# Nine-token rows for keys and values, per-head v transfers and a new order of the first chunk in a polysketch attention kernel

## The chip, the cores and the metric

The kernel runs on one core of a Trainium2 chip. The metric is device time in microseconds, from the start to the end of one execution; three runs of the kernel before gave 110.10, 110.65 and 111.04, a median of 110.65. A core has TensorE (PE in the profile, its weight loads apart as PEld), VectorE (DVE), ScalarE (ACT), GpSimd (POOL) and SyncE (SP), which here only issues transfers. Each engine works through its own instructions in the order of the program, and waits for the others through semaphores.

## What is computed

Two blocks follow each other. The first is attention with polynomial sketches, for 4 batches of 4 heads, 1088 tokens and 32 channels, with sketches of r = 8 rows:

```python
def phi(x):
    a = np.einsum('rd,bhsd->bhsr', S1, x)
    b = np.einsum('rd,bhsd->bhsr', S2, x)
    return np.einsum('bhsi,bhsj->bhsij', a, b).reshape(*x.shape[:-1], r * r)
q_p, k_p = phi(q), phi(k)
kv = np.einsum('bhsf,bhsd->bhfd', k_p, v)
z = np.sum(k_p, axis=2)
num = np.einsum('bhsf,bhfd->bhsd', q_p, kv)
den = np.einsum('bhsf,bhf->bhs', q_p, z)[..., None] + 1e-06
```

Its quotient num / den, with the heads side by side, is x, of 4 x 1088 x 128. The second block is x + relu(norm(x) @ w_ch1) @ w_ch2, where norm takes the mean and the deviation over 128 channels and scales by g_ln, and the hidden width is 512. All arrays are 32-bit floats on the chip, apart from S1, S2, w_ch1 and w_ch2, which arrive as 64-bit floats and are put together from their two 32-bit words by shifts, masks and float operations.

## The kernel before

**Layout.** A batch of q, k or v is seen as 128 rows of 34 tokens (4 heads x 32 rows, 34 = 1088 / 32), row by row on the partitions. q and k are loaded so (`load_rows`, L97), 544 KB a batch, the first batch of k in two pieces of 18 and 16 tokens. The 34 tokens of a row are cut into 9, 9, 8 and 8 (`ST`, `SN`), so that a batch's tokens, for one head, fill 9 tiles of 128, the last of them half empty. `turn_k` (L265) turns k by 32 x 32 blocks on VectorE into `kT`, channels on partitions; it works on two of the four cuts at a time. For batch 0 the four cuts lie on every fourth column (`step=4`), for later batches in blocks of 32. `load_v` (L104) brings v in the same order of tokens onto the partitions, by four transfers a batch, one a cut, each onto 32 partitions for all heads; a head has 10 tokens' room in a partition, and the ninth is zeroed first (L116).

**Sketches.** S1 and S2 are loaded sixteen times over, onto all 128 partitions (L79), one by ACT's queue and one by SP's. VectorE makes floats of them (`s_f`, L188 to L202); `sketches` (L279) makes `sk` for the keys and, by GpSimd, `sq` for the queries; `sketches2` (L293) makes `s2b`.

**Attention of a batch.** `key_features` (L308): matmuls of kT with sk, copied to `fs` by ACT. `key_products` (L327): the outer product of the two sketches, on GpSimd and for a third of batch 0 on VectorE. `key_sums` and `key_scale` (L337, L349) put the sum z into the query's sketch. `key_values` (L355): 36 matmuls of v with the products, nine tiles by four heads, head by head within a tile, so its first four need all heads of v. `key_rows` and `key_spread` (L365, L371) lay the result out as `kvr`. On the query's side: `turn_q`, `query_features`, `query_rows`, `quotients`, `query_products`, `query_turn`, then `numerators` (L454).

**Second block.** It goes by chunks of 512 tokens, two a batch, and a last one (8) of what is left over. `columns_of(c)` has x with channels on partitions; `send` stores it and `fetch` loads it back in rows for `stats` and the residual (chunk 0 is turned by TensorE instead, `turn_rows`). `hidden(c, j)` (L537), four a chunk, is a matmul with w1 and ACT's relu; `second(c, t)` (L548), four a chunk, has four matmuls with w2 each; `finish(c)` (L561) scales, adds x and stores.

**Weights.** The class `weight` (L210) makes floats of w1 and w2 in steps: `split` on VectorE (exponents and mantissa bits, `ex` and `bits`), `floats(0..3)` on ACT, `add` on GpSimd, `exps` on GpSimd (the exponents of W2), `signed` and `last` on VectorE. W1 is done in halves of 256, apart from its split and its step 3. `mean_free(a, bank)` (L580) is a matmul of `cg` and W1's half, which takes the mean out of w1; ACT copies the result to `w1`.

**Order.** Nothing is planned by a scheduler: the order is written out by hand, for chunk 0 from L583 on. `fill` (L162) is a matmul of ones that nobody reads, into the bank `XP` = `M[2]`, to keep TensorE going. The loads of batch 1 (L609 to L612) are released by a one-element copy into `kn[1]` on GpSimd (L608), which waits for `query_rows(0, 0, 4)`. In SP's queue the loads stand in the order S2, k (two), q, w1, v (four), w2, then k, q, v of batch 1 and k of batch 2, and from there on chunk by chunk between stores and fetches.

Of the kernel before, what the change touches and what calls it, by code (L numbers as in the profile page):

```python
# [25 lines left out]
def kernel(  # L26
# [29 lines left out]
    ST, SN = (0, 9, 18, 26), (9, 9, 8, 8)  # L56
# [13 lines left out]
    XP = M[2]  # L70
# [6 lines left out]
    s_raw = const([P, 2 * D], S1.dtype, "s_raw")  # L77
    for eng, src, a in ((act, S1, 0), (nc.sync, S2, D)):
        eng.dma_start(out=s_raw[:, a : a + D],  # L79
                      in_=bass.AP(src.tensor, src.offset, [[0, P // R], [D, R], [1, D]]))  # L80
# [7 lines left out]
    act.dma_start(out=g_row, in_=moe_g_ln.rearrange("(o p) -> o p", o=1))  # L88
# [3 lines left out]
    VH = 10 * D  # L92
# [4 lines left out]
    def load_rows(dst, src, b, t0=0, t1=G):  # L97
        nc.sync.dma_start(
            out=dst[b][:, D * t0 : D * t1],
            in_=bass.AP(src.tensor, src.offset + b * H * S * D + D * t0,  # L100
                        [[G * D, P], [1, D * (t1 - t0)]]),
        )

    def load_v(b):  # L104
        base = v.offset + b * H * S * D
        for r in range(4):
            n = SN[r] * D
            nc.sync.dma_start(
                out=_ap(vn[b], *((r, 32) if b == 0 else (32 * r, 32)), 0, [[VH, H], [1, n]],
                        step=4 if b == 0 else 1),  # L110
                in_=bass.AP(v.tensor, base + ST[r] * D, [[G * D, 32], [S * D, H], [1, n]]),
            )


    for t in vn:
        (dve if t is vn[0] else pool).memset(_ap(t, 0, P, 8 * D, [[VH, H], [1, D]]), 0.0)  # L116
    load_rows(kn, k, 0, 0, 18)
    load_rows(kn, k, 0, 18, G)
# [6 lines left out]
    )  # L125

# [19 lines left out]
    dve.tensor_tensor(out=m8, in0=bit, in1=head, op=ALU.is_equal)  # L146
    kT = [const([P, NT * P], F32, f"kT{i}") for i in range(2)]
    for t in kT:
        pool.memset(t[:, 8 * P :], 0.0)
# [38 lines left out]
    s_f = const([P, 2 * D], F32, "s_f")  # L188
    if s_raw.dtype == F32:
        dve.tensor_copy(out=s_f, in_=s_raw)  # L190
    else:
        t = exponent(s_raw, P, 2 * D, "s")
        split(t)
        act.activation(t["mant"], t["bits"], AF.Identity, bias=one, scale=2.0**-20)
        dve.tensor_scalar(out=t["exf"], in0=t["ex"], scalar1=-896.0, scalar2=0.0,
                          op0=ALU.add, op1=ALU.max)
        dve.tensor_scalar(out=t["e2"], in0=t["exf"], scalar1=255.0, scalar2=2.0**23,
                          op0=ALU.min, op1=ALU.mult)
        signed(t)
        dve.scalar_tensor_tensor(out=t["mant"], in0=t["lo"], scalar=2.0**-52, in1=t["mant"],  # L200
                                 op0=ALU.mult, op1=ALU.add)
        dve.tensor_tensor(out=s_f, in0=t["mant"], in1=t["e3"].bitcast(F32), op=ALU.mult)  # L202
# [7 lines left out]
    class weight:  # L210


        def __init__(self, dst, raw, tag):
            self.dst, self.raw, self.plain = dst, raw, raw.dtype == F32
            if not self.plain:
                self.t = exponent(raw, P, raw.shape[-1], tag)

        def cols(self, a, n):
            return {k: x[:, a : a + n] for k, x in self.t.items()}
# [17 lines left out]
        def exps(self, a=0, n=512):  # L237
            if not self.plain:
                t = self.cols(a, n)
                pool.tensor_scalar(out=t["exf"], in0=t["ex"], scalar1=-896.0, scalar2=0.0,  # L240
                                   op0=ALU.add, op1=ALU.max)
                pool.tensor_scalar(out=t["e2"], in0=t["exf"], scalar1=255.0, scalar2=2.0**23,
                                   op0=ALU.min, op1=ALU.mult)
# [18 lines left out]
    W1, W2 = weight(w1g, w1_raw, "w1"), weight(w2, w2_raw, "w2")  # L262


    def turn_k(b, r2):  # L265
        n = SN[r2]
        at, dims = (r2, [[1, 2], [P, n], [4, 32]]) if b == 0 else (
            32 * r2, [[32, 2], [P, n], [1, 32]])
        dve.transpose(  # L269
            _ap(kT[b % 2], 0, P, at, dims),  # L270
            _ap(kn[b], 0, P, D * ST[r2], [[D * n, 2], [D, n], [1, D]]),
        )
# [6 lines left out]
    def sketches():  # L279

        s_t = const([P, W], F32, "s_t")
        dve.transpose(s_t, s_f)
        dve.tensor_tensor(
            out=_ap(sk, 0, P, 0, [[HR, 2], [R, H], [1, R]]),
            in0=_ap(s_t, 0, P, 0, [[HR, 2], [R, H], [1, R]]),
            in1=_ap(m32, 0, P, 0, [[0, 2], [1, H], [0, R]]),
            op=ALU.mult,
        )
        for b in range(B):
            pool.tensor_copy(out=_ap(sq[b], 0, P, 0, [[R, 2], [1, R]]),  # L290
                             in_=_ap(s_t, 0, P, 0, [[HR, 2], [1, R]]))

    def sketches2():  # L293

        dve.tensor_tensor(
            out=_ap(s2b, 0, P, 0, [[D, H], [1, D]]),
            in0=_ap(s_f, 0, P, D, [[0, H], [1, D]]),
            in1=_ap(m8, 0, P, 0, [[1, H], [0, D]]),
            op=ALU.mult,
        )  # L300
# [279 lines left out]
    def mean_free(a, bank):  # L580
        pe.matmul(bank[:, 0:half], cg, w1g[:, a : a + half], start=True, stop=True)

    fill(2, XP, 512)  # L583
    turn_k(0, 0)
    sketches()
    turn_k(0, 2)
    fill(1, XP, 512)
    pe.matmul(FB[:, 64:65], g_row, one[0:1], start=True, stop=True)
    act.copy(g_col, FB[:, 64:65])
    pool.tensor_scalar(out=cg, in0=ident, scalar1=-1.0 / DM, scalar2=g_col,  # L590
                       op0=ALU.add, op1=ALU.mult)
    sketches2()
    key_features(0, 0, 4, M[0])
    key_features(0, 4, 9, M[1])
    key_products(pool, 0, 0, 4)
    turn_q(0, 0, 4)
    fill(1, XP, 256)
    key_sums(0, FB, 0)
    fill(1, XP)
# [3 lines left out]
    fill(1, XP)  # L603
    query_features(0, 0, 4)
    W1.split()
    query_rows(0, 0, 4)

    pool.tensor_copy(out=kn[1][:, 0:1], in_=fq[0][:, 0:1])  # L608
# [4 lines left out]
    W1.floats(3)  # L613
    W1.floats(2, 0, half)
    W1.add(0, half)
    W1.floats(0, 0, half)
    W1.floats(1, 0, half)
    W1.floats(0, half, half)
    quotients(0, 0, 4)
    fill(1, XP, 512)  # L620
    fill(1, XP, 256)
    key_values(0)
    key_rows()
    W1.floats(1, half, half)
    fill(1, XP, 256)
    key_spread(0, M[0], 0)
# [3 lines left out]
    query_turn(0, 2, 2)  # L630
    W1.signed(0, half)
    W1.last(dve, 0, half)
    W1.floats(2, half, half)
    W1.add(half, half)
    W2.floats(3)
    fill(1, XP, 512)
    numerators(0, 0, 4)
    columns_of(0)
    mean_free(0, M[0])
    act.copy(w1[:, 0:half], M[0][:, 0:half])  # L640
    W1.signed(half, half)
    W1.last(dve, half, half)
    W2.split()
    W2.exps()
    turn_q(0, 4, 4)
    W2.floats(2)
    fill(1, XP)


    pool.memset(kT[0][:, 8 * P + 64 :], 0.0)  # L650
    hidden(0, 0)
    W2.add()
    mean_free(half, FB)
    act.copy(w1[:, half:], FB[:, 0:half])
    query_features(0, 4, 4)
    hidden(0, 1)
    W2.signed()
    query_rows(0, 4, 4)
    turn_k(1, 0)
    W2.last(dve)  # L660
    turn_rows(0)
# [3 lines left out]
    turn_k(1, 2)  # L665
# [31 lines left out]
    turn_k(2, 0)  # L697
    turn_k(2, 2)
# [33 lines left out]
    for b in range(1, 4):  # L732
# [37 lines left out]
        if b < 2:  # L770
            turn_k(b + 2, 0)
            turn_k(b + 2, 2)
# [78 lines left out]
```

## Time and profile before

| what | value |
|---|---|
| median of three runs | 110.65 us (110.10 to 111.04) |
| profiled execution | 110.73 us, of which the span from first to last instruction is 108.9 us |
| instructions in it | 3605 |
| granted TensorE clock | 0.996 of full speed |
| bytes read and written in HBM | 9.77 MB, 4.19 MB |
| DMA issue to landing, median: q, k, v, w | 5.5, 6.3, 5.1 (v's larger pieces), 6.6 us |
| first chunk: `key_values(0)`, numerators, `hidden(0,0)`, `second(0,0)` start at | 13.12, 17.17, 19.31, 25.88 us |

All times of the profile are microseconds from the span's start. In a line of the profile stand the engine, the line of the kernel, the operation, the tile written and the tiles read, the shape, and how often; in brackets the idle time of the engine before it and what ended it. A row of digits cuts the span into 40 slices of 2.7 us, with the busy share of each in tenths. A matmul of 32-bit floats appears as two records. The engine lists count busy time only; transfers are listed by queue, with their packets.

### The profile page before, as it was taken

To read this page: it belongs to the slowest core of one execution; us is meant where nothing else is said; L and a number is where in the kernel's file an instruction comes from. 1 tells how busy PE (TensorE), PEld (TensorE's weight loads), DVE (VectorE), ACT (ScalarE), POOL (GpSimd) and SP (SyncE) were. 2 spreads that over 40 slices of the span, in tenths; PEclk is the share of its full clock that TensorE was granted. 3 is DMA by queue.
4 is the path that set the end of the run, shared out by engine and by line. 5 is a ranking of instruction groups with operands and counts; after the bars stand their busy time and mean duration, and the time that the engine had idled before them with its cause. 6 is when DMAs were issued, how large, how long until landed. Compare 5 with 4: busy or idle time off the path is not lost. (4 is left out here: it accounts for less than half of the span.)

```text
span 108.9 us, 3605 instructions
## 1 busy us (share of the span) xinstructions
PE 100.2 (92%) x1496; PEld 67.3 (62%) x1496; DVE 70.9 (65%) x204; ACT 39.2 (36%) x79; POOL 53.9 (49%) x67
## 2 busy tenths in 40 slices
PE   6949996994999999999999999999999999999890
PEld 3317545445973677836963786559449658849680
DVE  5496989349859958789879703896950493274411
ACT  4103693662222532434316511451282251071220
POOL 7036682992997397672960693059340034016000
PEclk9999999999999999999999999999999999999998
DMA  1999159910002595334495862520036450132031
GB/s 24 251 332 360 62 174 341 264 45 3 6 0 102 155 303 149 143 106 124 82 355 181 204 211 76 152 56 17 3 76 219 122 163 11 48 91 53 0 96 48
DMA packets 12162, 14.19 MB, mean 130 GB/s; under 512 B 2417, under 2 KB 8946, under 8 KB 12146
## 3 DMA queue, kind: packets, MB, share of 16 engines
q1 hardware_dynamic: 11856, 13.87, 42.8%
q8 instruction: 11, 0.18, 0.7%
q10 hardware_dynamic: 290, 0.10, 0.3%
q14 instruction: 5, 0.04, 0.1%
HBM read 9.77 MB, written 4.19 MB: 128 GB/s over the span
## 5 line engine op out<-in xcount | busy, mean ns | idle before, releaser
L552 PEld LDWEIGHTS M<-w,hT 128*128 128x128 f32 x256 | 31.0, 191 | 7.7 <-issue 3.8
L552 PE MATMUL M<-w,hT 128*128 128x128 f32 x256 | 34.3, 281 | 1.5 <-DVE w L260 1.4
L542 PE MATMUL M<-xT,w 128*128 128x512 f32 (+1 forms) x72 | 34.2, 588 | 0.7 <-DVE ob L564 0.5
L544 ACT ACTIVATE hT<-M 128x512 f32<-128x512 f32 (+1 forms) x36 | 20.6, 574 | 33.7 <-PE M L542 33.7
L432 POOL TENSOR_TENSOR qp<-a,fq 128x1024 f32<-128x1024 f32 (+1 forms) x9 | 16.2, 1816 | 20.0 <-DVE a L425 20.0
L564 DVE SCALAR_TENSOR_TENSOR ob<-M,rstd,x 128x128 f32<-128x128 f32 x32 | 9.0, 344 | 16.5 <-PE M L552 7.1
L542 PEld LDWEIGHTS M<-xT,w 128*128 128x128 f32 x72 | 11.9, 189 | 9.9 <-issue 6.6
L330 POOL TENSOR_TENSOR kp<-fs 128x1024 f32<-128x1024 f32 (+2 forms) x8 | 16.2, 2036 | 2.2 <-ACT fs L324 1.4
L443 DVE STREAM_TRANSPOSE qpT<-qp 128x1024 f32<-128x1024 f32 (+1 forms) x10 | 10.8, 1082 | 4.0 <-POOL qp L432 3.9
L164 PE MATMUL M<-ones 128*128 128x512 f32 (+2 forms) x22 | 10.5, 591 | 1.1 <-DVE ones L86 1.1
L524 POOL TENSOR_SCALAR va<-mv 128x4 f32<-128x4 f32 (+1 forms) x9 | 2.1, 229 | 15.8 <-DVE mv L517 15.6
L526 POOL TENSOR_TENSOR rstd<-va,mhalf 128x4 f32<-128x4 f32 (+1 forms) x9 | 9.0, 1000 | 0.7
L461 PE MATMUL X<-qpT,kvr 32*32 32x256 f32 (+2 forms) x384 | 7.5, 323 | 1.0 <-DVE qpT L443 1.0
L515 DVE BATCH_NORM_STATS2 st<-x 128x6 f32<-128x128 f32 x34 | 7.4, 279 | 0.3
L461 PEld LDWEIGHTS X<-qpT,kvr 32*32 32x32 f32 x384 | 4.5, 103 | 4.4 <-ACT loww L235 1.8
L269 DVE STREAM_TRANSPOSE kT<-kn 128x576 f32<-128x576 f32 (+1 forms) x8 | 6.4, 822 | 1.0 <-DMA kn<-in_k_dram 1.0
L476 ACT COPY xT<-X 128x512 f32<-128x512 f32 (+1 forms) x8 | 4.2, 561 | 7.7 <-PE X L461 7.7
L164 PEld LDWEIGHTS M<-ones 128*128 128x128 f32 x22 | 4.4, 226 | 4.1 <-issue 2.7
L409 DVE STREAM_TRANSPOSE fq<-X 128x512 f32<-128x512 f32 (+1 forms) x9 | 5.8, 669 | 1.0 <-PE X L399 1.0
L507 DVE STREAM_TRANSPOSE x<-xx 128x512 f32<-128x512 f32 (+1 forms) x8 | 5.4, 669 | 0.8 <-DMA xx<-xd 0.8
L358 PEld LDWEIGHTS FB<-kp,vn 128*32 128x32 f32 x288 | 4.2, 110 | 2.6 <-POOL kp L330 1.5
L387 DVE STREAM_TRANSPOSE qT<-qn 128x1024 f32<-128x1024 f32 (+1 forms) x5 | 5.1, 1015 | 0.6 <-DMA qn<-in_q_dram 0.6
(100 smaller groups left out, 85.5 us busy)
## 6 DMA issues: line engine op xcount, KB each, us to landing
qn<-in_q_dram SPq DMA_DIRECT2D x4, 544.0 KB, 5.5
out_dram<-ob SPq DMA_DIRECT2D x33, 64.0 KB, 1.8
xd<-xT SPq DMA_DIRECT2D x7, 256.0 KB, 2.6
xx<-xd SPq DMA_DIRECT2D x28, 64.0 KB, 2.0
kn<-in_k_dram SPq DMA_DIRECT2D x3, 544.0 KB, 6.3
vn<-in_v_dram SPq DMA_DIRECT2D x8, 144.0 KB, 5.1
w_raw<-in_moe_w_ch_dram SPq DMA_DIRECT2D x2, 512.0 KB, 6.6
vn<-in_v_dram SPq DMA_DIRECT2D x8, 128.0 KB, 5.8
```

Of the source, the lines that this page charges most:

```text
L164: pe.matmul(bank[:, 0:w], ones, _ap(ones, 0, P, 0, [[0, w // P], [1, P]]), start=True, stop=True)
L269: dve.transpose(_ap(kT[b % 2], 0, P, at, dims), _ap(kn[b], 0, P, D * ST[r2], [[D * n, 2], [D, n], [1, D]]),)
L330: eng.tensor_tensor(out=_ap(o, 0, P, H * F * t0, [[F, (t1 - t0) * H], [R, R], [1, R]]), in0=_ap(a, 0, P, at, [[R, (t1 - t0) * H], [1, R], ...
L432: eng.tensor_tensor(out=_ap(qp[p, t0 // 4], 0, P, H * F * (t0 % 4), [[F, m], [R, R], [1, R]]), in0=_ap(a2s[p], 0, P, HR * t0, [[R, m], [1, ...
L443: dve.transpose(_ap(qpT[p], 0, P, 32 * t0, [[32, n], [width(p), 8], [1, 32]]), qp[p, t0 // 4][:, o : o + n * H * F],)
L461: pe.matmul(X[D * h : D * h + D, 512 * r + 32 * t0 : 512 * r + 32 * (t0 + n)], kvr[p if p < 4 else r][rows, DM * i + D * h : DM * i + D * ...
L515: dve.bn_stats(out=st[:, 6 * t : 6 * t + 6], in_=x[c][:, P * t : P * (t + 1)])
L526: pool.tensor_tensor(out=rs[:, 0:n], in0=va[:, 0:n], in1=mhalf[:, 0:n], op=ALU.pow)
L542: pe.matmul(hp[:, 0:n], w1[:, P * j : P * (j + 1)], xT[c][:, 0:n], start=True, stop=True)
L544: act.activation(_ap(hT[c], 0, P, 512 * j, dims), hp[:, 0:n], AF.Relu)
L552: pe.matmul(po[c][:, DM * t : DM * (t + 1)], hT[c][:, 512 * j + P * t : 512 * j + P * (t + 1)], w2[:, DM * j : DM * (j + 1)], start=(j == ...
L564: dve.scalar_tensor_tensor(out=ob[c][:, P * t : P * (t + 1)], in0=po[c][:, P * t : P * (t + 1)], scalar=rstd[c][:, t : t + 1], in1=x[c][:, ...
```

## The change

- **Rows of nine tokens.** All four cuts of a row are nine tokens: 0 to 8, 9 to 17, 18 to 26 and 27 to 35. The last has only seven of its own; for v the other two are read from what follows, and `kT` is zero there (its padding is now two tiles of 32 columns, zeroed once). Batch 0 has the same layout as the others, and k of batch 0 comes by one transfer. `turn_k` takes ranges of cuts and tokens.
- **v by heads.** `load_v` has one transfer a head, onto all 128 partitions; its source is 4 cuts x 32 rows x 288 numbers. For the last head of the last batch it is two transfers, and the piece that would be read past the end is zeroed instead. The other zeroing of v is gone.
- **Sketches.** S1 and S2 go onto every fourth partition (32 in all), both by SP's queue, after a memset of `s_raw` on GpSimd; the conversion is 32 wide instead of 64. `s2b` now needs S on each partition, which a matmul with a new 0/1 matrix `pick` (made by a GpSimd iota and one VectorE comparison) puts into `M[2]`. g's load moves behind ACT's table load, its matmul to just before.
- **W1 in halves.** `split` and step 3 of W1 are done by halves too; for the first half `ex` and `bits` lie in the PSUM bank `M[0]`. W2's `exps` go to VectorE, the copy of w1's first half too.
- **Order of chunk 0.** Fills go to X, and those between `query_features(0)` and `key_values(0)` are gone. `cg` is made later. The copy that releases batch 1's loads is on ACT, behind `key_spread(0)`, and waits for the quotients. `mean_free` of the second half and `turn_k(1)` stand later, W2's steps earlier.

```diff
-    VH = 10 * D
+    VH = NT * D
...
     def load_v(b):
-        base = v.offset + b * H * S * D
-        for r in range(4):
-            n = SN[r] * D
-            nc.sync.dma_start(
-                out=_ap(vn[b], *((r, 32) if b == 0 else (32 * r, 32)), 0, [[VH, H], [1, n]],
-                        step=4 if b == 0 else 1),
-                in_=bass.AP(v.tensor, base + ST[r] * D, [[G * D, 32], [S * D, H], [1, n]]),
-            )
+        for h in range(H):
+            at = v.offset + (b * H + h) * S * D
+            parts = [(0, 3, NT), (3, 4, 7)] if (b, h) == (B - 1, H - 1) else [(0, 4, NT)]
+            for r0, r1, n in parts:
+                nc.sync.dma_start(
+                    out=_ap(vn[b], 32 * r0, 32 * (r1 - r0), VH * h, [[1, D * n]]),
+                    in_=bass.AP(v.tensor, at + r0 * NT * D,
+                                [[NT * D, r1 - r0], [G * D, 32], [1, D * n]]),
+                )
...
-    for eng, src, a in ((act, S1, 0), (nc.sync, S2, D)):
-        eng.dma_start(out=s_raw[:, a : a + D],
-                      in_=bass.AP(src.tensor, src.offset, [[0, P // R], [D, R], [1, D]]))
+    pool.memset(s_raw.bitcast(U32), 0)
+    for src, a in ((S1, 0), (S2, 1)):
+        nc.sync.dma_start(out=_ap(s_raw, a, H * R, 0, [[1, D]], step=4),
+                          in_=bass.AP(src.tensor, src.offset, [[0, H], [D, R], [1, D]]))
...
-    load_rows(kn, k, 0, 0, 18)
-    load_rows(kn, k, 0, 18, G)
+    load_rows(kn, k, 0)
...
+            if self.bank is not None and a == 0:
+                y = self.bank.bitcast(U32)
+                t["ex"], t["bits"] = y[:, 0:n], y[:, n : 2 * n]
...
-                pool.tensor_scalar(out=t["exf"], in0=t["ex"], scalar1=-896.0, scalar2=0.0,
-                                   op0=ALU.add, op1=ALU.max)
+                dve.tensor_scalar(out=t["exf"], in0=t["ex"], scalar1=-896.0, scalar2=0.0,
+                                  op0=ALU.add, op1=ALU.max)
...
-    def turn_k(b, r2):
+    def turn_k(b, r0, r1, t0, t1):
+        n = t1 - t0
         dve.transpose(
-            _ap(kT[b % 2], 0, P, at, dims),
-            _ap(kn[b], 0, P, D * ST[r2], [[D * n, 2], [D, n], [1, D]]),
+            _ap(kT[b % 2], 0, P, 32 * r0 + P * t0, [[32, r1 - r0], [P, n], [1, 32]]),
+            _ap(kn[b], 0, P, D * (NT * r0 + t0), [[D * NT, r1 - r0], [D, n], [1, D]]),
         )
```

The order of chunk 0 after the change, from its first fill to `hidden(0, 0)`:

```python
    fill(2, X, 512)
    sketches()
    turn_k(0, 0, 4, 0, 4)
    dve.tensor_scalar(out=pick, in0=away, scalar1=0, scalar2=None, op0=ALU.is_equal)
    turn_k(0, 0, 3, 4, 9)
    turn_k(0, 3, 4, 4, 7)
    fill(1, X, 256)
    key_features(0, 0, 4, M[0])
    key_products(pool, 0, 0, 4)
    turn_q(0, 0, 4)
    pe.matmul(M[2][:, 64:65], g_row, one[0:1], start=True, stop=True)
    sketches2(M[2])
    key_features(0, 4, 9, M[1])
    fill(1, X)
    key_sums(0, FB, 0)
    fill(1, X)
    key_scale(0, FB, 32)
    key_products(pool, 0, 4, 6)
    key_products(dve, 0, 6, 9, M[1], 4)
    W1.split(0, half)
    fill(1, X)
    query_features(0, 0, 4)
    W1.floats(3, 0, half)
    query_rows(0, 0, 4)
    for step in (2, 0, 1):
        W1.floats(step, 0, half)
...
    quotients(0, 0, 4)
    key_values(0)
    key_rows()
    W1.floats(3, half, half)
    fill(1, X, 256)
    key_spread(0, M[1], 0)
    act.copy(kn[1][:, 0:1], a2s[0][:, 0:1])
    load_rows(kn, k, 1)
    load_rows(qn, q, 1)
    load_v(1)
    load_rows(kn, k, 2)
    query_products(0, pool, 2, 2)
    query_products(0, dve, 0, 2)
    query_turn(0, 0, 2)
    query_turn(0, 2, 2)
    W1.add(0, half)
    W1.signed(0, half)
    W1.last(dve, 0, half)
    W1.split(half, half)
    W2.floats(3)
    fill(1, X, 512)
    fill(1, X, 256)
    numerators(0, 0, 4)
    columns_of(0)
    for step in (2, 0, 1):
        W1.floats(step, half, half)
    mean_free(0, M[0])
    dve.tensor_copy(out=w1[:, 0:half], in_=M[0][:, 0:half])
    turn_q(0, 4, 4)
    W1.add(half, half)
    W2.split()
    W1.signed(half, half)
    W1.last(dve, half, half)
    W2.exps()
    W2.signed()
    fill(1, M[2])
    hidden(0, 0)
```

## The prediction

> **What bounds the kernel now.** I read the busy times first, then the chain of waits, then the timeline from the start to 30 us, the windows of 1 us over the same stretch, and the DMA lists.
>
> ```profile
> PE 100.2 (92%) x1496; PEld 67.3 (62%) x1496; DVE 70.9 (65%) x204; ACT 39.2 (36%) x79; POOL 53.9 (49%) x67
> PE   6949996994999999999999999999999999999890
> ```
>
> TensorE is the bound. From 25.88 us on its timeline has hardly a hole, so whatever delays or advances the stretch before it moves the end by the same amount. The chain of waits starts only at 102.77 us and says nothing of the head; the head is where the change works. Its timeline:
>
> ```profile
> 13.12 1.21 PE L358 MATMUL FB<-kp,vn 128*32 128x64 f32 x72
> 16.31 0.71 DVE L443 STREAM_TRANSPOSE qpT<-qp 128x512 f32<-128x512 f32 x1 [0.22 <-POOL qp L432]
> 17.17 1.06 PE L461 MATMUL X<-qpT,kvr 32*32 32x128 f32 x64 [1.04 <-DVE qpT L443]
> 19.31 1.13 PE L542 MATMUL M<-xT,w 128*128 128x512 f32 x2 [0.24 <-ACT w L640]
> 25.88 2.02 PE L552 MATMUL M<-w,hT 128*128 128x128 f32 x16 [1.36 <-DVE w L260]
> 27.83 1.27 PE L315 MATMUL X<-sk,kT 128*64 128x64 f32 x36
> ```
>
> `key_values(0)` runs at 13.12, behind fills and not behind v. The numerators wait for VectorE's second transpose (done 17.02), `hidden(0,0)` for the first half of w1 (19.31), `key_features(1)` starts at 27.83. I follow 19.31: from there to 27.83 are 8.5 us.
>
> **The start.** S1 moves from ACT's queue to SP's, behind a new GpSimd memset (0.72 us, about 0.2 us by the memset rows), and k becomes one transfer. By the 0.69 and 0.64 us of SP's issues k goes out at about 2.2 instead of 1.46, but q and w1 only 0.1 later. S lands at 4.0 instead of 3.1; the conversion (1.3 us) and `sk` are done by 5.8, before k (6.4), so k hides them; without that cover they would cost 0.9. The first turn writes whole blocks: 0.71 us as L269 in its later runs, against 1.20 here. First features at 7.2 instead of 8.00. The rest of kT (two turns, 0.9 us), `pick` (0.2 to 0.3), `turn_q` (q lands at 8.6 as now, 0.71) and `s2b` (0.27) bring VectorE to 9.6, where its key products stood at 9.77: the 0.8 is mostly lost again. The `pick` matmul and g's move onto M2 lie in TensorE's holes.
>
> **W1.** Its two splits took 0.78 and 1.30 us at 512 wide beside GpSimd's products; W2's, with less beside them, 0.42. For a half written to PSUM I bound one at 0.21 to 0.65 and take 0.42. So 2.08 becomes 0.85, and the transpose of the query features goes from 12.56 to about 11.45. Quotients end at 13.5, GpSimd's products (1.58) at 15.1, the second transpose at 15.9: 1.15 us earlier. Copying w1's half by VectorE instead of ACT is 0.37 for 0.37. W2's exponents leave GpSimd (2.05 + 1.94) for VectorE (0.42 to 0.78 each), which removes the 1.36 us wait at 25.88. But then ACT is late next: hT0, hT1, W2's mantissa 0.72, x 0.58, w1's half 0.37, hT2, hT3 stand in one queue, and VectorE has the second quotients and k's last turn. Added up from these rows, `hidden(0,0)` to `key_features(1)` is 8.4 to 8.5 us after the change too. The head is thus won or lost by where `hidden(0,0)` starts.
>
> With v in time the numerators go at 15.9, end at 16.95, `mean_free` and the copy take 1.0: `hidden(0,0)` at 17.95, 1.35 us early.
>
> **v.** Before, four transfers each read 32 rows x 4 heads x 1152 or 1024 bytes; after, a transfer's source is written 4 blocks x 32 rows x 1152 bytes, and only the SBUF side counts 128. How many DMA engines carry it is not shown, so I bound it. Each engine that takes part adds a packet of its own at the end, as the queues' totals show:
>
> ```profile
> q1 hardware_dynamic: 11856, 13.87, 42.8%
> q10 hardware_dynamic: 290, 0.10, 0.3%
> ```
>
> Queue 10 is ACT's: S1 has 128 pieces, the last store 128, g_row one; 290 - 257 = 33 = 16 + 16 + 1. The transfers whose outer counts are 16 and 128 used 16 engines, the one with outer count 1 used one. On queue 1, 101 transfers with outer counts of 16, 32 or 128 have 10,240 pieces, and 11,856 - 10,240 = 101 x 16. So the number follows the outer count somehow; for 4 the ends are 4 and 16 engines. I take 4, since an outer count of 1 gave exactly that number, and the same four for all heads: the rows do not tell which, and one queue serving the same kind of transfer four times running is the plainer case.
>
> The Trainium skill, "DMA: Bandwidth & Descriptors", section on why a DMA increments its semaphore by 16, says so outright and against this change: a DMA from SP runs on the largest number up to 16 that divides the slowest dimension of both sides, and on the lowest-numbered engines. By it all four heads share the same four; the trace agrees as far as it goes (33 and 1,616), and has no count of 4.
>
> What 4 engines cost:
>
> ```profile
> 8.00:9.00 1.00, 1.00 (x34) 1.00 (x36) 0.43 (x2) 0.27 (x1) 0.00 (x0) 1.00 1.02 361
> 9.00:10.00 1.00, 1.00 (x29) 0.60 (x26) 0.57 (x2) 0.53 (x2) 0.81 (x1) 1.00 1.06 365
> w_raw<-in_moe_w_ch_dram SPq DMA_DIRECT2D x2, 512.0 KB, 6.6
> ```
>
> The last two columns are the busy share of 16 engines and GB/s: 361 / 16 / 1.02 is 22 GB/s an engine, in the stretch that carries v. v of one batch is 4 x 128 x 1152 = 590 KB, 147 KB on each of four engines, 6.6 us. They first carry their share of k, q and w1 (1.64 MB): by the windows' GB/s the sum is reached at 8.1 us; w1's last piece lands 6.6 after its issue at 3.26, at 9.9 (6.6 is the last column of the list of DMA issues). With 0.5 for the later start, v lands between 15.2 and 17; I take 16.0. `key_values(0)` waits for it, and TensorE's whole queue behind it, from about 11.4. ACT's queue behind `kvT` waits too, in it the copy that now releases SP's loads of k, q, v of batch 1 (13.67 before, 18.8 now); k1 is due at about 27 and lands 4 to 8 us after issue, so this stays covered.
>
> From 16.0: key_values 1.2, kvT 0.4, spread 0.45, two fills 1.4, numerators 1.06, `mean_free` and copy 1.0: `hidden(0,0)` at 21.5, **2.2 us late**. v must land by about 12.2 to cost nothing and by 13.5 for no change; even 15.2 is past that.
>
> Later loads: v1 (due 35) and v2 are early. v3 is issued at 59.34, two microseconds ahead of chunk 4's store (61.33), whose rows on those engines then queue until about 67.5; the fetch goes at 69.3 instead of 65.57 and lands at 73, where `rows_of(4)` is due at 71.81. VectorE has 0.3 to 0.7 us of slack there, and the numerators of batch 3 follow at 77.50. Bounds 0 and 1.2, I take **0.5**, with a little at chunk 2 in it. The zeroing of less padding and the batch-1 turns of other widths change nothing off the head.
>
> **Sum**: 2.2 + 0.5 = 2.7 us on a span of 108.9, which is 111.6. The profiled execution took 110.73, 1.8 more than its span and 0.1 over the median of 110.65: 113.4 predicted.
>
> **Rivals.**
> - *All 16 engines carry v* (the SBUF side's 128 decides, or each head goes to another four). v lands at 11.5 to 12 as now, `hidden(0,0)` at 17.95: 108.9 - 1.35, time **109.3**. The decisive point is v's landing, 13.5 us. For it: no row has a count of 4. The windows from 18 to 21 us also show today's v of batch 1, written to 32 adjacent partitions a transfer, at 227 to 275 GB/s with the engines full; all partitions would mend that, but off the path.
> - *Four engines, and TensorE's clock falls in the wait.* The first three fills are six passes in 5.16 us, 0.86 each, where L542 later averages 0.59 at the same width: after idling it started slow. TensorE would stand from 11.4 to 16.0. If it is slow again, fills, spread and `mean_free` after the wait (some 3 us of work) take up to 3 more, 0 at the other end; at 1.8 the time is **115.2**. Against: the holes of 1.5 us before 8.00 and 1.0 before 17.17 left no trace. In the Trainium skill, "TensorE: Matmul & The Clock Gate", part 1, the clock halves after an idle window of about 3.4 us that runs freely, and a wait of 4.6 us may or may not hold one; no run here shows a wait so long.
> - *v is late but hidden*, landing at about 13.5 (eight engines): 110.6, no change.
>
> **How the numbers follow.** Four engines with the clock kept 0.45 (112.2 to 114.6), with the clock lost 0.22, all engines 0.25 (108.6 to 110), hidden 0.08. The likeliest gives 113.4. The range, 109.2 to 115.8, leaves out the lower half of the 16-engine case and the top of the slow-clock case. A measurement here tells about 1% (110.1 to 111.04 in three runs). Slower by over 1%: 0.67; faster 0.22, since 109.3 is just past 1% and part of that case falls inside; same 0.11.
>
> **What would show it.** In the changed profile: L367 starting near 16 us after some 4 us of idle TensorE put down to the DMA of vn; windows from 11 to 16 us at a quarter of DMA share and near 90 GB/s; vn's landing at 8 to 12 us instead of 5 to 6; queue 1 with fewer small packets than 16 a transfer. The L418 transpose before 12 us and `hidden(0,0)` at about 21.5 test the rest. I am wrong if L367 starts before 13 us, or if 19.31's successor moves without the end moving with it.

## The result, and the profile after

The changed kernel takes **115.67 us** (median of four runs, 115.22 to 117.97); the kernel before took 110.84 us beside it (four runs, 110.10 to 112.11). The ratio is **1.0445, 95% interval 1.0361 to 1.053**: slower by about 4.5%. The forecast was 113.4. Both kernels have some runs in which TensorE's clock comes up late and which are longer; medians are of all runs, ratios leave the disturbed ones out.

The profiled execution took 115.84 us, its span is 113.9 (108.9 before). Its page, the lines that answer to those shown of before, with the row of the granted clock:

```profile
PE 103.1 (90%) x1496; PEld 70.1 (62%) x1496; DVE 70.3 (62%) x210; ACT 38.9 (34%) x80; POOL 48.9 (43%) x63
PE   6949739985999999999999999999799999999890
PEclk9996555999999999999999999999999999999999
q1 hardware_dynamic: 11463, 13.97, 39.2%
q10 hardware_dynamic: 146, 0.07, 0.2%
```

TensorE does the same number of instructions, and from the eighth slice on its row is nearly as full as before, apart from a 7 in the 29th. The head has a hole (a 3 in the sixth slice), and the clock row reads 5 in three slices. The timeline of TensorE, from the query features to the keys of batch 1 (columns: start, time, engine, line, operation, tiles, shape, count, and the idle time before it with what ended it):

```profile
12.76 0.96 PE L367 MATMUL FB<-kp,vn 128*32 128x64 f32 x4
14.94 0.42 PE L367 MATMUL FB<-kp,vn 128*32 128x64 f32 x2 [1.22 <-DMA vn<-in_v_dram]
16.40 2.13 PE L367 MATMUL FB<-kp,vn 128*32 128x64 f32 x66 [1.04 <-DMA vn<-in_v_dram]
...
21.06 1.07 PE L470 MATMUL X<-qpT,kvr 32*32 32x128 f32 x64
...
23.37 1.10 PE L551 MATMUL M<-xT,w 128*128 128x512 f32 x2 [0.39 <-DVE w L648]
...
28.00 1.98 PE L551 MATMUL M<-xT,w 128*128 128x512 f32 x4 [1.17 <-ACT w L669]
29.82 2.23 PE L561 MATMUL M<-w,hT 128*128 128x128 f32 x16
31.98 1.27 PE L324 MATMUL X<-sk,kT 128*64 128x64 f32 x36
```

`key_values(0)` comes in pieces, each waiting for the DMA of v: its first tile goes head by head as the heads land, the last at 16.40. The 66 records that are left (33 matmuls) then take 2.13 us, where the whole step of 72 took 1.21 before. `hidden(0,0)` starts at 23.37 instead of 19.31 (4.06 late), `key_features(1)` at 31.98 instead of 27.83 (4.15 late). So 4.1 of the 5.0 us of span are lost ahead of `hidden(0,0)`, the rest later, below. The windows of 1 us (stretch; PE, PEld, DVE, ACT, POOL busy; granted clock; DMA share; GB/s) tell why:

```profile
9.00:10.00 1.00, 1.00 (x18) 0.71 (x15) 0.28 (x2) 0.42 (x1) 1.00 (x1) 0.60 0.27 96
10.00:11.00 1.00, 1.00 (x21) 0.86 (x20) 1.00 (x2) 0.18 (x1) 1.00 (x2) 0.50 0.31 100
...
15.00:16.00 1.00, 0.36 (x2) 0.12 (x2) 0.93 (x3) 0.00 (x0) 0.83 (x1) 0.50 0.27 97
...
19.00:20.00 1.00, 1.00 (x5) 0.64 (x4) 0.00 (x0) 0.39 (x2) 0.00 (x0) 0.78 0.00 0
```

While v is on its way the DMA share is a quarter and the rate 94 to 100 GB/s, both in the stretch from 14 to 16 us and already at 9 to 11: four engines at about 24 GB/s each. (At 11 to 13 us, between them, the rate was 258 to 259 GB/s; by the order of SP's queue that is w2, issued behind v.) And the clock was halved from 9.2 to 19.4 us; it fell while TensorE was in its key features, well ahead of the wait for v.

The packet count says four exactly. Queue 1 of the changed kernel has 102 transfers with 10,048 pieces. 11,463 - 10,048 = 1,415 small packets, where 16 a transfer would be 1,632: 217 too few. Four engines carry 15 whole heads (15 x 12 = 180 too few) and S1 and S2, whose source has four heads too (24); three engines carry the piece of 96 partitions (13). 180 + 24 + 13 = 217.

### The profile page after: what moved, and what is told of

Its sections match the earlier page's. It is cut to its first block, busy times and chain, and to the rows that moved or that the text cites. A ratio compares the mean times of both kernels' runs of the same rounds, so it can differ in the third digit from the quotient of the medians.

```text
span 113.9 us, 3604 instructions
## 1 busy us (share of the span) xinstructions
PE 103.1 (90%) x1496; PEld 70.1 (62%) x1496; DVE 70.3 (62%) x210; ACT 38.9 (34%) x80; POOL 48.9 (43%) x63
## 3 DMA queue, kind: packets, MB, share of 16 engines
q1 hardware_dynamic: 11463, 13.97, 39.2%
## 5 line engine op out<-in xcount | busy, mean ns | idle before, releaser
L441 POOL TENSOR_TENSOR qp<-a,fq 128x1024 f32<-128x1024 f32 (+1 forms) x9 | 16.2, 1813 | 23.6 <-DVE a L434 23.6
L166 PE MATMUL X<-ones 128*128 128x512 f32 (+2 forms) x18 | 9.6, 667 | 1.1 <-DVE span L130 1.1
L367 PE MATMUL FB<-kp,vn 128*32 128x64 f32 x288 | 7.0, 244 | 2.4 <-DMA vn<-in_v_dram 2.3
L367 PEld LDWEIGHTS FB<-kp,vn 128*32 128x32 f32 x288 | 5.6, 125 | 5.7 <-DMA vn<-in_v_dram 3.1
L533 POOL TENSOR_SCALAR va<-mv 128x4 f32<-128x4 f32 (+1 forms) x9 | 2.1, 229 | 16.2 <-DVE mv L526 16.0
L166 PEld LDWEIGHTS X<-ones 128*128 128x128 f32 x18 | 4.5, 291 | 3.9 <-issue 2.5
L260 POOL TENSOR_TENSOR mantw<-mantw,loww 128x256 f32<-128x256 f32 (+1 forms) x3 | 2.7, 905 | 9.1 <-ACT mantw L241 9.1
```

The lines of the kernel that those rows point to most:

```text
L166: pe.matmul(bank[:, 0:w], ones, _ap(ones, 0, P, 0, [[0, w // P], [1, P]]), start=True, stop=True)
L367: pe.matmul(FB[D * h : D * h + D, 64 : 64 + F], vn[b][:, VH * h + D * t : VH * h + D * (t + 1)], kp[b % 2][:, H * F * t + F * h : H * F * ...
L441: eng.tensor_tensor(out=_ap(qp[p, t0 // 4], 0, P, H * F * (t0 % 4), [[F, m], [R, R], [1, R]]), in0=_ap(a2s[p], 0, P, HR * t0, [[R, m], [1, ...
```

## The experiments

### v on four engines or on sixteen

**v_by_cuts** gives the 16 engines back and changes nothing else:

```diff
-        for h in range(H):
-            at = v.offset + (b * H + h) * S * D
+        for r in range(4):
...
-                    out=_ap(vn[b], 32 * r0, 32 * (r1 - r0), VH * h, [[1, D * n]]),
-                    in_=bass.AP(v.tensor, at + r0 * NT * D,
-                                [[NT * D, r1 - r0], [G * D, 32], [1, D * n]]),
+                    out=_ap(vn[b], 32 * r, 32, VH * h0, [[VH, h1 - h0], [1, D * n]]),
+                    in_=bass.AP(v.tensor, v.offset + (b * H + h0) * S * D + r * NT * D,
+                                [[G * D, 32], [S * D, h1 - h0], [1, D * n]]),
```

> The changed kernel with v alone put back to transfers by cut (source 32 rows x 4 heads x 1152 bytes, outer count 32 on both sides), everything else as changed, the nine-token layout too. Theory 'four engines carry v': v of batch 0 lands by 12.5 us instead of 16.4, key_values(0) starts before 13.2 without a wait for vn, queue 1 has 16 small packets for each transfer again, and the batch-2 fetch is back at 4 us or less after its store. hidden(0,0) then starts at 19.0 to 20.5 (23.37 in the changed kernel, 19.31 before): the time falls to 110.5 to 112. Rival 'the slow TensorE clock from 9.2 to 19.4 us is the main cost': the time stays above 114, since nothing ahead of 9.2 us changes.

Measured: 112.95 us (four runs, 111.75 to 113.33), ratio 1.0166 (1.0071 to 1.0261). Queue 1 has 11,656 packets, 24 short of 16 a transfer, which are S1 and S2. So 2.7 us come back, but less than expected, and the profiled run (span 111.3) shows why:

```profile
14.36 2.16 PE L366 MATMUL FB<-kp,vn 128*32 128x64 f32 x72
```

v is in time (no wait in brackets), but the same 72 records take 2.16 us instead of 1.21: here TensorE was slow from the start of the kernel to 17.3 us. The slow clock is a second matter, to be set apart before anything else is measured.

### The clock

Three runs change the width of one fill: **third_fill_512** and **v_by_cuts_fill_512** make the last one ahead of the key features 512 wide again, as it was before; **before_fill_256** does the opposite to the kernel before.

```diff
-    fill(1, X, 256)
+    fill(1, X, 512)
     key_features(0, 0, 4, M[0])
```

> The changed kernel with the third fill of the head 512 wide again, as before the change, and nothing else; fills compute nothing that is used. Theory 'the shorter fill lets the clock fall': the granted clock stays at 1.0 past 9.2 us. Whether it then falls at about 16 us, in the wait for v (12 to 16.4), tells two cases apart: if it holds, key_values(0) takes 1.2 instead of 2.1 us, hidden(0,0) starts at 21.5 and the time is 113.8; if the wait makes it fall, hidden(0,0) stays at 22.5 to 23.5 and the time within 1 us of 115.7. Rival 'something else in the head lets it fall' (the later features, the operand of the fills): the clock falls at 9.2 as now and the time is the same.

Measured: 116.20 (four runs, 115.82 to 116.67), ratio 1.048 (1.0401 to 1.0559): no gain. In its profile the clock is full through the key features and falls at 14.1 us, now in the wait for v, and `key_values` is slow just the same (v's last head came 1 us sooner here, at 15.38):

```profile
15.38 2.13 PE L367 MATMUL FB<-kp,vn 128*32 128x64 f32 x66 [1.11 <-DMA vn<-in_v_dram]
```

> Both at once: v by cuts and the third fill 512 wide. Theory 'four engines and the lost clock are all that the change costs': the clock is 1.0 throughout, hidden(0,0) starts at about 18.0 and the time is 109 to 110, under the kernel before (110.8). If other parts of the change cost something too, 110.5 or more with hidden(0,0) at 19 or later.

Measured: 112.42 (four runs), but from 110.5 to 112.66. The profiled run is the one of 110.5, at full clock, with `hidden(0,0)` at 18.98; the others had a mean granted clock of 0.969 to 0.985.

> The kernel before with its third fill 256 wide instead of 512, nothing else. Theory 'the shorter fill lets the clock fall': the granted clock falls to 0.5 at 9.2 us here too, the fills of 11.6 us take twice as long and key_values(0) moves from 13.1 to 14.5 or later; the time grows by 1 to 2 us. Rival 'the clock falls for another reason in the changed kernel': the clock stays at 1.0 and the time at 110.8 within 0.5.

Measured: 112.56 (110.4 to 113.52), ratio 1.0023 (0.9882 to 1.0163). The fastest run equals the fastest of the kernel before beside it (110.47); in the profiled one, of 113.52, TensorE was slow up to 17.5 us, and `hidden(0,0)` started at 22.19. So the width of this fill shows no cost of its own; whether it changes how often the clock comes up late, four runs can't tell. And the kernel before has the same trouble: beside the later experiments its runs went from 110.2 to 114.0.

What ended it in two kernels is a little more work in the head. **before_busy** adds one fill of 256 columns to the kernel before; **v_by_cuts_busy** has v by cuts, a fill of 512 and the one of 256 ahead of the key features, and one fill of 512 ahead of `key_values`:

```diff
+    fill(1, X, 512)
     fill(1, X, 256)
     key_features(0, 0, 4, M[0])
...
+    fill(1, M[2], 512)
     key_values(0)
```

> The kernel before with one more fill of 256 behind its third of 512 in the head, which closes half of TensorE's hole ahead of 8 us. Theory 'runs of the kernel before between 111.9 and 113.4 are runs in which the clock came up late': all runs within 110.3 to 111.2. Rival: the spread stays.

Measured: 110.51 (ten runs, 110.23 to 110.81), ratio 0.9963 (0.9924 to 1.0002). The long runs are gone.

> v by cuts (outer count 32), the same longer head fills and one fill of 512 into M2 ahead of key_values(0). Theory 'with v on 16 engines and TensorE busy the change costs nothing': every run at full clock from 8 us on, time 110 to 111 with a spread under 1 us, hidden(0,0) at 18.5 to 19.5. If the runs still spread up to 112.6, the clock does not follow from the fills.

Measured: **110.46** (ten runs, 110.26 to 110.58), ratio 0.9958 (0.9916 to 1.0000). Its TensorE timeline:

```profile
12.99 1.21 PE L366 MATMUL FB<-kp,vn 128*32 128x64 f32 x72
...
16.78 1.06 PE L469 MATMUL X<-qpT,kvr 32*32 32x128 f32 x64 [0.35 <-DVE qpT L451]
...
19.07 1.10 PE L550 MATMUL M<-xT,w 128*128 128x512 f32 x2 [0.39 <-DVE w L649]
```

and that of before_busy:

```profile
12.87 1.21 PE L358 MATMUL FB<-kp,vn 128*32 128x64 f32 x72
...
16.90 1.06 PE L461 MATMUL X<-qpT,kvr 32*32 32x128 f32 x64 [1.02 <-DVE qpT L443]
...
19.05 1.12 PE L542 MATMUL M<-xT,w 128*128 128x512 f32 x2 [0.24 <-ACT w L641]
```

The two stand at `hidden(0,0)` at 19.07 and 19.05. More fill is not a sure remedy: with the same head fills, v_by_heads_rows_first below has one run of ten at 114.18 (mean granted clock 0.967) and last_v_by_heads one of twelve at 113.98 (0.985).

These two runs are the ground for what follows: with the clock quiet and v on 16 engines, **all the rest of the change is worth nothing that can be measured** (110.46 against 110.51).

### Is it the number of transfers, or the order of their counts?

**v_by_heads_rows_first** keeps one transfer a head onto all 128 partitions, but its source counts 32 rows of 4 cuts instead of 4 cuts of 32 rows. The cuts then lie on every fourth partition, and `kT` is written to every fourth column to match; the fills are those of v_by_cuts_busy.

```diff
-                    in_=bass.AP(v.tensor, at + r0 * NT * D,
-                                [[NT * D, r1 - r0], [G * D, 32], [1, D * n]]),
+                    in_=bass.AP(v.tensor, at, [[G * D, 32], [NT * D, 4], [1, D * NT]]),
...
-            _ap(kT[b % 2], 0, P, 32 * r0 + P * t0, [[32, r1 - r0], [P, n], [1, 32]]),
+            _ap(kT[b % 2], 0, P, r0 + P * t0, [[1, r1 - r0], [P, n], [4, 32]]),
```

> One transfer a head onto all 128 partitions as in the change, but its source is written 32 rows x 4 cuts x 1152 bytes instead of 4 cuts x 32 rows: token cut r of row i then lies on partition 4i + r, and the turns of k write every fourth column to match. Only the order of two counts differs, and the turns (about 0.5 us more on VectorE for each batch, by the 1.20 us of such a turn before the change). Head fills and one fill of 512 as in the run by cuts. Theory 'the outer count sets the engines': 16 small packets a transfer, v of batch 0 lands by 12 us, hidden(0,0) at 18 to 19.5, time 109.5 to 111. Rival 'a transfer by head onto 128 partitions is slow in itself': v lands after 15 us and the time is 114 or more.

Measured: 111.66 (ten runs, 111.56 to 114.18), ratio 1.0074 (1.0034 to 1.0114). Queue 1 has 11,688 packets: 104 transfers now (the padded last head goes in four), 10,048 + 104 x 16 - 24 = 11,688, so every v transfer is on 16 engines. The first two transfers of batch 0 land at 9.7 and 10.1 us, where those of v_by_cuts_busy land at 11.0 and 11.7, and `key_values(0)` does not wait for v. So the order of the two counts decides, and not the number of transfers. From 8 to 11 us the windows have 271 to 379 GB/s, against 219 to 235 in v_by_cuts_busy: one transfer a head onto 128 partitions, with the long count first, was even the quicker way here. Its time over v_by_cuts_busy is not v's. The turns of k into every fourth column are slower: those of batch 0 take 1.08 us and 1.19 for two (0.71 and 0.83 there), and `hidden(0,0)` is 0.28 late; those of a later batch take 2.17 instead of 1.36, and `key_features(1)` waits 0.51 us for one. From there to the last `hidden` (103.79 against 102.93) the kernel runs some 0.85 us behind.

### Which v costs what

**four_engines_busy_wait** is the changed kernel with v by heads throughout, but with five fills of 512 in front of `key_values(0)` so that TensorE stays busy through the wait.

```diff
+    fill(1, X, 512)
     fill(1, X, 256)
...
+    fill(5, M[2], 512)
     key_values(0)
```

> The changed kernel, v by heads as it is, with TensorE kept busy: the head's third fill is 512 and then 256 wide, and five fills of 512 into M2 stand between query_features(0) and key_values(0); fills compute nothing that is used. This is the prediction's likeliest case, four engines with the clock kept. Theory 'v lands at about 16.4 and the slow clock comes from TensorE standing': the clock is at full speed from 8 us on, key_values(0) starts at 16.4 to 17 and takes 1.2, hidden(0,0) starts at 21.5 to 22, the span is 3 to 3.5 over the kernel before and the time 113.5 to 114.3. Rival 'the clock falls whatever TensorE does there': key_values(0) still takes 2.1 and the time stays at 115.5 or more.

Measured: 116.19 (four runs, 114.81 to 117.46), ratio 1.0509 (1.0386 to 1.0633). The profiled run is the 114.81, with the clock full from the key features on. The timeline of its TensorE:

```profile
11.82 4.56 PE L166 MATMUL M<-ones 128*128 128x512 f32 x10
16.31 1.39 PE L367 MATMUL FB<-kp,vn 128*32 128x64 f32 x72
...
22.12 1.10 PE L551 MATMUL M<-xT,w 128*128 128x512 f32 x2 [0.39 <-DVE w L650]
...
60.74 1.49 PE L470 MATMUL X<-qpT,kvr 32*32 32x256 f32 x64 [1.13 <-DVE qpT L452]
```

`hidden(0,0)` is 3.05 us behind that of v_by_cuts_busy with no slow clock, and a second wait of 1.13 us stands at 60.74, at the first numerators of batch 2; together they are the 4.2 us by which its span is longer. The other three runs were longer than forecast, and no trace shows why. Five fills at half clock would take 4.6 us more, an estimate from their 4.56 here.

Two runs divide v between its batches. **first_v_by_heads** has only v of batch 0 by heads, with the five fills (`load_v` takes the transfers by heads for `b == 0` and those by cuts for the others):

> v of batch 0 by heads as in the change, batches 1 to 3 by cuts, with TensorE kept busy through the wait (five fills of 512). The other half of the same split: hidden(0,0) at 21.5 to 22.5, no stall later; where the clock is up from the head on, the time is 113.0 to 113.8, 2.6 to 3.3 over the run by cuts. Runs in which the clock comes up late are longer, up to 115.5, since the fills then take twice their time.

Measured: 113.72 (four runs, 113.44 to 114.25), ratio 1.025 (1.0179 to 1.0320), which is 3.26 over v_by_cuts_busy.

```profile
16.29 1.21 PE L375 MATMUL FB<-kp,vn 128*32 128x64 f32 x72
...
21.95 1.10 PE L559 MATMUL M<-xT,w 128*128 128x512 f32 x2 [0.39 <-DVE w L658]
```

`hidden(0,0)` is 2.88 us late, and no numerators wait later on. One thing to mind: `key_values(0)` starts right behind the fills here, with no wait for v in brackets. The DMA rate is 96 GB/s from 15 to 16 us and 16 GB/s from 16 to 17, so v was complete at about 16.2 (an estimate); the fills hide its landing and add next to nothing to it. And 0.42 of the 3.3 us by which the span is longer than that of v_by_cuts_busy is lost at 47.5 to 48.1, for no reason that the profile names.

**later_v_by_heads** is the opposite, batch 0 by cuts and the other three by heads:

> v of batch 0 by cuts, v of batches 1 to 3 by heads as in the change, with the head fills and the fill of 512 of the run by cuts (110.46). What is added to that run is the later loads on four engines alone. Theory 'chunk stores queue behind v on those engines': a stall of TensorE at the numerators of batch 2 or 3 of 0.8 to 1.2 us, behind a transpose that waits for a fetch; time 111.3 to 111.8. Rival 'the later loads are hidden, the stall came from the head's lateness': 110.3 to 110.8, within the run by cuts.

Measured: 112.01 (ten runs, 111.29 to 113.75), ratio 1.0076 (1.0022 to 1.0129): 1.55 over v_by_cuts_busy by the medians, 1.3 by the ratios. Its profiled run does not settle where. v of batch 0, by cuts as there, happened to land later (128 GB/s in the window from 9 to 10 us, 219 in v_by_cuts_busy): `key_values(0)` waited 1.38 us for it, `hidden(0,0)` came 1.0 late, and the numerators of batch 3 wait only 0.19 us.

**last_v_by_heads** leaves only v of batch 3 by heads, the place that the prediction had named (against later_v_by_heads):

```diff
-        if b == 0:
+        if b < B - 1:
             for r in range(4):
```

> v of batches 0, 1 and 2 by cuts, v of batch 3 alone by heads (five transfers, the padded last cut on its own); the fills of v_by_cuts_busy. It asks where the 1.0 to 1.5 us of later_v_by_heads come from. Theory A, the prediction's place: v of batch 3 stands ahead of the stores and fetches of chunk 4's rows on four engines, so the fetch xx lands late, VectorE's turn of it and behind it the second qpT of batch 3 are late, and the numerators of chunk 4 stall. Then most of the cost remains: median 111.0 to 111.8, VectorE's transpose of xx at about 73 to 75 waits 1 us or more for the DMA, and the numerators near 77 stand up to 1 us. Rival B: the cost of later_v_by_heads lay elsewhere (its profiled run had v of batch 0 land 1.4 us later than v_by_cuts_busy, and 0.2 us at the numerators of batch 3), in v of batches 1 and 2 or in the landing of v of batch 0 from run to run: then 110.3 to 110.7, no stall at batch 3, and key_values(0) at 13.0 again.

Measured: 111.41 (twelve runs, 110.42 to 113.98), ratio 1.0033 (0.9989 to 1.0077): 0.95 over v_by_cuts_busy by the medians, 0.8 by the ratios, as theory A had it. It differs from run to run: the lowest, 110.42, is within the runs of v_by_cuts_busy. The profile, of a run of 111.8, shows it step by step. SP's queue of v_by_cuts_busy, the store and the fetch of chunk 4:

```profile
62.82 0.85 SPq L491 DMA_DIRECT2D xd<-xT  x2
65.20 3.97 SPq L498 DMA_DIRECT2D xx<-xd  x8
```

of last_v_by_heads:

```profile
62.74 0.84 SPq L500 DMA_DIRECT2D xd<-xT  x2
69.86 4.88 SPq L507 DMA_DIRECT2D xx<-xd  x8
```

then VectorE's timeline, and TensorE's, of the same run:

```profile
74.30 0.71 DVE L524 STREAM_TRANSPOSE x<-xx 128x512 f32<-128x512 f32 x1 [2.34 <-DMA xx<-xd]
```

```profile
78.60 1.48 PE L478 MATMUL X<-qpT,kvr 32*32 32x256 f32 x64 [0.96 <-DVE qpT L460]
```

The store goes out at the same time, but its rows on four engines stand behind v of batch 3, and the fetch that waits for it goes 4.66 us later. VectorE then stands 2.34 us for the rows of x, its transposes of the query products are behind that, and TensorE waits 0.96 us. At the end the span is 1.2 us longer (0.22 of it from the head). The changed kernel has the same: its chunk-4 store at 66.76, the fetch only at 73.77, VectorE waiting 2.16 us, its last transpose of the query products done at 82.35, and the numerators at 82.49 after a wait of 0.78. (The profile puts this wait down to a copy by ACT done at 82.41; in v_by_cuts_busy the same numerators start 0.96 after the `hidden` ahead of them and wait for no such copy, so VectorE is the likelier cause.)

### One try for a faster kernel

In v_by_cuts_busy, as in the changed kernel, `hidden(0,2)` waits 1.18 us for the second half of w1. **w1_half_sooner** moves W2's mantissa step on ACT and GpSimd's sum for W2 in front of `hidden(0,1)`, and `mean_free` of the second half and its copy in front of the transposes of `turn_rows`; otherwise it is v_by_cuts_busy.

```diff
     hidden(0, 0)
+    W2.floats(2)
+    W2.add()
     query_features(0, 4, 4)
     hidden(0, 1)
-    W2.floats(2)
-    W2.add()
+    mean_free(half, FB)
+    act.copy(w1[:, half:], FB[:, 0:half])
...
-    mean_free(half, FB)
-    act.copy(w1[:, half:], FB[:, 0:half])
```

> The run by cuts (110.46), with ACT's queue reordered: W2's mantissa step goes between hidden(0,0) and hidden(0,1), into 0.9 us in which ACT waits, and mean_free of the second half with the copy of w1's half stands before turn_rows(0). Theory 'TensorE's 1.18 us wait for w1's half (and the same wait in the changed kernel) is ACT's queue alone': the wait shrinks to under 0.4 us, second(0,0) starts at 24.1 to 24.6 instead of 25.5, and the time is 109.3 to 109.9, under both kernels. Rival 'k's last turn or w2 on VectorE is late next': second(0,0) or key_features(1) waits instead and the time stays at 110.2 to 110.6.

Measured: 110.55 (twelve runs, 110.22 to 111.23), ratio 0.9957 (0.9917 to 0.9997): no better than v_by_cuts_busy. TensorE's timeline:

```profile
22.95 1.98 PE L550 MATMUL M<-xT,w 128*128 128x512 f32 x4
25.46 2.02 PE L560 MATMUL M<-w,hT 128*128 128x128 f32 x16 [0.53 <-DVE w L267]
27.80 1.27 PE L323 MATMUL X<-sk,kT 128*64 128x64 f32 x36 [0.32 <-DVE kT L275]
```

and one line of VectorE's:

```profile
21.87 1.52 DVE L249 TENSOR_SCALAR e2w<-exfw 128x512 uint32<-128x512 f32 x1
```

The wait of 1.18 is gone at 22.95, but two new ones stand behind it, for w2 and for k's turn, both late on VectorE: this step of W2's exponents took 1.52 us beside GpSimd's sum, which now runs at the same time (21.84 to 23.11), and 0.43 in v_by_cuts_busy. `key_features(1)` is at 27.80 against 27.69 there.

## Why the prediction was right, and where its sizes were off

The direction and the main mechanism were right: v by heads goes over four engines, `key_values(0)` waits for it, and the head moves the end. The likeliest case was not what happened, though: it kept the clock, and the clock was lost. By the spans, the profiled run of the changed kernel is 5.1 us behind v_by_cuts_busy (113.9 and 108.8), and it divides so: v of batch 0 on four engines 2.88 (first_v_by_heads at `hidden(0,0)`), slow clock 1.42 (23.37 against 21.95 there), stall at batch 3 0.84 (the numerators at 82.49 against 77.36, 5.13, less 4.29 at batch 2). By the medians the whole is 5.2, v of batch 0 3.26, v of batch 3 0.95, and what is left for the clock is 1.0; no run measures the clock alone.

- **Four engines** (right). I chose 4 of 4 to 16, the same four for all heads; 217 missing packets and 94 to 100 GB/s say so. The Trainium skill, "DMA: Bandwidth & Descriptors", section on why a DMA increments its semaphore by 16, has the rule (largest number up to 16 that divides the slowest dimension of both sides); the trace agrees here for a slowest count of 4, 3 and, in v_by_heads_rows_first, 32.
- **v lands at 16.0** (right): the last head at 16.4, and at 15.38 in third_fill_512.
- **What v costs at `hidden(0,0)`** (right within 0.7): from v in time to v on four engines I had 17.95 to 21.5, 3.55; measured 19.07 to 21.95, 2.88, and 3.26 in the medians (with the five fills, whose end and v's landing fall together there).
- **The head with v in time gains 1.35** (wrong; the largest error of the first sum). It gains nothing: `hidden(0,0)` is at 19.07 in v_by_cuts_busy and at 19.05 in before_busy, and the time is 110.46 where I gave this rival 109.3. Of the steps: first features 7.2, measured 7.56, since k came later and its first turn began at 6.79, not 6.4 (in the changed kernel itself they started at 7.24); the splits of W1 0.85, measured 0.42 + 0.43, right. But the transpose of the query features, forecast at 11.45, came at 12.17, as v_by_cuts_busy's VectorE shows:

```profile
10.12 0.96 DVE L338 TENSOR_TENSOR kp<-M,fs 128x768 f32<-128x768 f32 x1 [0.72 <-ACT fs L332]
11.00 0.42 DVE L179 TENSOR_SCALAR M<-w_raw 128x256 uint32<-128x256 uint32 x1
11.45 0.43 DVE L181 TENSOR_SCALAR M<-w_raw 128x256 uint32<-128x256 uint32 x1
12.17 0.72 DVE L417 STREAM_TRANSPOSE fq<-X 128x512 f32<-128x512 f32 x1 [0.29 <-PE X L407]
```

  I had added up VectorE's own steps. Its products wait 0.72 us for ACT's `fs`: the new order has the key features in two parts on TensorE, with the matmuls of g and `pick` between them. And the transpose waits 0.29 for TensorE, which had no hole there any more. The second transpose ends at 16.63 (forecast 15.9), and from the numerators to `hidden(0,0)` it is 2.29, not 2.05. Of the 1.35 against 19.31, 1.12 were lost in these steps (0.72 up to the transpose, 0.16 at the numerators, 0.24 behind them); the 0.24 that were left, before_busy has as well. Some of this stood in the rows of before: the numerators start 0.15 after the second transpose (17.02 to 17.17), and it is 2.14 from there to `hidden(0,0)`. The sum had 0 and 2.05, which is how 1.15 at the transpose became 1.35.
- **`hidden(0,0)` to `key_features(1)` 8.4 to 8.5** (right): 8.61 in the changed kernel, 8.62 in v_by_cuts_busy. The wait that went came back, as said, behind ACT: 1.17 us for w1's second half.
- **Later loads 0.5, bounds 0 and 1.2** (place right, size half): forecast a fetch at 69.3; last_v_by_heads has it at 69.86, and the cost is 0.8 to 0.96. The slack that I gave VectorE, 0.3 to 0.7, was not enough. The place is not fixed: in four_engines_busy_wait the stall stood at batch 2, not at batch 3.
- **The clock 0** in the likeliest case (wrong; 1.0 to 1.4). The rival with the slow clock had 1.8 for it, 115.2 in all, and comes nearest to the measured 115.67. That is luck in part: it took too much for the clock, and it too counted on the 1.35 that did not come. And its reason holds only in part: in third_fill_512 the clock fell in the wait, in the profiled run of the changed kernel it fell at 9.19, before the wait began. What made it fall there was not settled.

Put together: 113.4, plus 1.1 for the gain that did not come, plus 0.45 at batch 3, plus 1.0 for the clock, less 0.3 for v, is 115.7. This is no check, since the 1.0 is what the other terms left; the 1.42 from the spans is the only other figure for it.

Of the signs, L367 was to start near 16 after some 4 us of idle TensorE. It started at 12.76, with the first two heads' matmuls (four records), and by my own words ("wrong if it starts before 13") this would have spoken against me. The sign was badly put: its first tile goes head by head, and what waited for v's last head was the rest. Two others failed through the slow clock: the query transpose, to come before 12 us, came at 13.02 after 1.46 us of waiting for TensorE, and `hidden(0,0)` came at 23.37 and not at 21.5.

## What to carry to other kernels

Before rearranging a load, look at the first count of its source and its destination, and compare the queue's packets with pieces plus 16 a transfer: a missing dozen per transfer means four engines, and here cost some 3 us on the first load. Load onto all partitions with the long count first, or in slices of partitions; but look at who has to read the new layout. When a gain is added up on one engine, go through the other engines that feed it at their new places, since the step after the one that was shortened waits for them.

And before a difference of 1% is measured, see whether the kernel's own runs fall into groups: here one more fill of 256 columns in the head brought a spread of 3.8 us down to 0.6, without which the rest of this change could not have been told from nothing.

## What was unexpected

**The clock of the head differs from run to run of the same kernel.** By the clock records in the packed traces TensorE's clock came up between 4.5 and 7.3 us in most profiles, but at 17.3 us in that of v_by_cuts and at 17.5 in that of before_fill_256; and it fell back in between in two (9.2 to 19.4 in the changed kernel, 14.1 to 20.9 in third_fill_512). One more fill of 256 columns took the kernel before from 110.2 to 114.0 down to 110.23 to 110.81.

The Trainium skill, "TensorE: Matmul & The Clock Gate", part 1, has a window of about 3.4 us that runs freely. In the changed kernel the clock was low for 10.24 us, three such windows, which agrees; in third_fill_512 it was low for 6.83, two of them. But the page's remark that the loss is less than 1% of a typical kernel does not hold here: with the clock up at 17.5 us, `hidden(0,0)` was 2.9 us late (22.19 against 19.31), 2.6% of the kernel.

What counts as busy in such a window was not settled. Idle time does not tell: ahead of the key features TensorE was idle for 1.46 us in the profile before, 0.24 in before_busy and 1.13 in v_by_cuts_busy, and the last two have no long run; but from 5.8 to 9.2 us it was busy 1.96 us in the changed kernel, where the clock then fell, and 1.94 in the profile before, where it held.

**The row of the granted clock can hide it.** In the page of v_by_cuts it reads 9 in each slice, while the 72 records of `key_values(0)` took 2.16 us instead of 1.21: where the kernel starts slow, the durations of its instructions tell it, and the row does not.

**v's landing on 16 engines is not fixed either.** With the same four transfers for batch 0, TensorE did not wait for v in v_by_cuts_busy (12.99) and waited 1.38 us for it, up to 14.41, in later_v_by_heads. What slowed it there was not settled.
